# An MLP kernel whose first weight chunks work on two half blocks of tokens, with the LayerNorm statistics shared between two engines

## The chip, the cores and the metric

The kernel runs on one core of a Trainium2 chip. The metric is the time of one execution on the device, in microseconds (us), as the median of several executions. The engines are named as the profile names them: PE is TensorE, DVE is VectorE, ACT is ScalarE, POOL is GpSimd and SP is SyncE, which here only issues transfers.

## The reference

A block of a channel MLP: LayerNorm without gain or offset, a matrix product with W1, a bias and a tanh-approximated gelu, a second product with W2 and a bias. All inputs are bf16, with 2048 tokens, 1024 features and 3584 hidden features.

```python
def _layernorm(x, axis=-1, eps=1e-5):
    m = jnp.mean(x, axis=axis, keepdims=True)
    v = jnp.var(x, axis=axis, keepdims=True)
    return (x - m) / jnp.sqrt(v + eps)

def reference(x, w1, b1, w2, b2):
    y = _layernorm(x, axis=-1)
    h = _gelu(jnp.einsum("bsd,df->bsf", y, w1) + b1)
    return jnp.einsum("bsf,fd->bsd", h, w2) + b2
```

## The kernel before

The tokens are worked on in two blocks of 1024. Both matrix products use Strassen's scheme in Winograd's form: a product of 2 x 2 sub-matrices takes seven half-size products in place of eight, at the price of sums of the operands (S1 to S4 of the input, T1 to T4 of the weights), which DVE makes, and of sums of the results. A small list scheduler in the kernel file assigns a fixed order to each engine when the program is built; the priorities in the code are the scheduler's, and the chip runs the resulting order.

Before PE can work on the first block, each of its eight tiles of 128 tokens must go through this chain: load, statistics and scaling on DVE (with a power on POOL), eight transposes on PE, two copies out of PSUM by ACT.

```python
        def ln(s, i, prio, gate=()):
            st = [add("DVE", 0.68, lambda e, k=k: e.bn_stats(st_sb[:, i, 6 * k:6 * k + 6],
                                                             x_sb[:, i, k * HT:(k + 1) * HT]),
                      (x_ld[(s, i)][k], *gate), prio + 0.001 * k, f"st{s}_{i}_{k}") for k in range(2)]
            ag = add("DVE", 0.21, lambda e: e.bn_aggr(mv_sb[:, i, :], st_sb[:, i, :]), st, prio + 0.002, f"mv{s}_{i}")
            vp = add("DVE", 0.15, ...)                       # variance + eps
            rs = add("POOL", 0.55, ... op=ALU.pow ...)       # to the power -1/2
            y_ok[(s, i)] = add("DVE", 0.56, ...)             # (x - mean) * rstd, in fp16
```

The sums of the input combine tokens 0 to 511 with tokens 512 to 1023 (A1x and A2x below), so S1 to S4 wait for the last tile. Until then PE can do only the products that need no sum, P1 = A11 x W1 quarter and P2 = A12 x W1 quarter, and the kernel does them tile by tile for three units of 256 hidden features and whole for two more.

```python
            S1 = tt("S1", "A21", "A22", ALU.add, a21 + a22, ())
            S2 = tt("S2", "S1", "A11", ALU.subtract, a11, (S1,))
            S3 = tt("S3", "A11", "A21", ALU.subtract, a11 + a21, (S1,))
            S4 = tt("S4", "A12", "S2", ALU.subtract, a12, (S2,))
        # ...
                if p in (1, 2) and s == 0 and u < WAVE_UNITS:
                    o = None
                    for t in range(TH):
                        # 4 matmuls of 128 columns as soon as tile t is there
        # ...
        for i in range(NT):
            ln(0, i, -100 + 2.3 * i)
            pe_T(0, i, -60 + 2.3 * i)
```

Of the kernel before, what the change touches and what calls it, by code (L numbers as in the profile page):

```python
# [22 lines left out]
LN_EPS = 1e-5  # L23
# [7 lines left out]
OPEN_UNITS = 5  # L31
WAVE_UNITS = 3

MM512 = 0.2163
MM128 = 0.0585
# [35 lines left out]
class Planner:  # L71
# [3 lines left out]
    SLACK = {"PE": 0.35, "ACT": 0.1, "DVE": 0.1, "POOL": 0.1, "SP": 0.05}  # L75
# [9 lines left out]
    def place(self):  # L85
# [12 lines left out]
        while left:  # L98
# [46 lines left out]
            for u in o.users:  # L145
                u.waiting -= 1
                u.ready = max(u.ready, o.end + LAT)
                if u.waiting == 0:
                    avail.append(u)
# [43 lines left out]
def bass_standalone__mixer_channel_mlp__prompt_kernel(  # L193
# [24 lines left out]
    with ExitStack() as es:  # L218
# [47 lines left out]
        T_HEAD = 16.0  # L266
# [25 lines left out]
        def load_w1(s, c, prio):  # L292
            n = s * NC + c
            deps = w1_use.get(n - N_W1, ())
            w1_ld[(s, c)] = [dma(w1_sb[:, n % N_W1, j * KH:(j + 1) * KH, :],
                                 w1v[:, j * KH:(j + 1) * KH, c * 4 * P:(c + 1) * 4 * P], deps, prio + 0.01 * j,
                                 f"w1_{s}_{c}_{j}", f"w1_{n % N_W1}_{j}", KH * P * 4 * P * 2) for j in range(2)]
# [17 lines left out]
        load_x(0, 0, (), 0.0, halves=True, eng=("SP", "ACT"))  # L315
        load_x(0, 1, (), 0.1, halves=True, eng=("ACT", "ACT"))
        load_x(0, 2, (), 0.2)
        b1_ld = dma(b1r_sb[:, :], b1.rearrange("(t p) -> t p", p=P), (), 0.3, "b1", "b1", F * 2)
        load_w1(0, 0, 0.4)
        load_x(0, 3, (), 0.5)  # L320
        load_w1(0, 1, 0.6)
        for i in range(4, NT):
            load_x(0, i, (), 0.7 + 0.01 * i)
        load_w1(0, 2, 0.9)
        b2_ld = dma(b2_sb[:, :], b2.partition_broadcast(P), (), 30.0, "b2", "b2", P * D * 2)


        def warm(n, deps, prio):
# [5 lines left out]
        add("ACT", 1.3, lambda e: e.preload_act_table(ACT.Gelu_apprx_tanh), (), 1.0, "table")  # L334
# [3 lines left out]
                                                    identity=identb[0:FT, 0:FT]), ())], (c_idb, b1_ld), -4.0, "b1t",  # L338
                  alloc=hold_b)
        b1c = add("ACT", 0.2, lambda e: e.copy(out=b1_sb[:, :], in_=ps16[:, hold_b.k, 0:FT].bitcast(BF16)), (b1t,), 2.0,  # L340
                  "b1c", frees=(hold_b,))


        y_ok = {}
        x_free = {}

        def ln(s, i, prio, gate=()):
# [4 lines left out]
            vp = add("DVE", 0.15, lambda e: e.tensor_scalar(out=vpe_sb[:, i:i + 1], in0=mv_sb[:, i, 1:2],  # L352
# [8 lines left out]
            return st  # L361

# [5 lines left out]
        def pe_T(s, i, prio, gate=()):  # L368
# [7 lines left out]
            for k in range(2):  # L376
                res.append(add("ACT", 0.59, lambda e, k=k: e.copy(  # L377
                    out=dst_y(i, k), in_=ps16[:, hold.k, k * HT:(k + 1) * HT].rearrange("p (j s) -> p j s", j=KH)),
                    (tr, *gate), prio + 0.05 * k, f"te{s}_{i}_{k}", frees=(hold,) if k else ()))
            res[1].deps.append(res[0])  # L380
            y_in[(s, i)] = res

        def dma_T(s, i, prio, gate):
            res = []
            for k in range(2):
                res.append(add("SP", 0.45, lambda e, k=k: e.dma_start_transpose(
                    dst_y(i, k), x16[:, i, k * HT:(k + 1) * HT]), (y_ok[(s, i)], *gate[k]), prio + 0.05 * k,
                    f"yt{s}_{i}_{k}", sem=f"d_yt{i}{k}", inc=16, nbytes=P * HT * 2))
# [3 lines left out]
        ys = {}  # L392

        def y_sums(s, prio, gate=()):

            t1 = [y_in[(s, i)] for i in range(TH)]
            t2 = [y_in[(s, i)] for i in range(TH, NT)]
            a11, a12 = [[t[k] for t in t1] for k in range(2)]
            a21, a22 = [[t[k] for t in t2] for k in range(2)]

            def tt(n, x0, x1, op, deps, dp):
                res = []
                for g in range(2):
                    sl = slice(g * KH // 2, (g + 1) * KH // 2)
                    res.append(add("DVE", 0.62, lambda e, sl=sl: e.tensor_tensor(  # L405
                        out=yop[n][:, sl, :], in0=yop[x0][:, sl, :], in1=yop[x1][:, sl, :], op=op),
                        [*deps, *gate] + [d[g] for d in dp], prio + {"S1": 0, "S2": 1, "S3": 2, "S4": 3}[n] + 0.1 * g,
                        f"y{n}_{s}_{g}"))
                return res

            S1 = tt("S1", "A21", "A22", ALU.add, a21 + a22, ())
            S2 = tt("S2", "S1", "A11", ALU.subtract, a11, (S1,))
            S3 = tt("S3", "A11", "A21", ALU.subtract, a11 + a21, (S1,))
            S4 = tt("S4", "A12", "S2", ALU.subtract, a12, (S2,))
            rep = lambda l: [l[0]] * (KH // 2) + [l[1]] * (KH - KH // 2)
            ys[s] = {"S1": rep(S1), "S2": rep(S2), "S3": rep(S3), "S4": rep(S4)}
            for n, l in (("A11", a11), ("A12", a12), ("A22", a22)):
                ys[s][n] = l
# [6 lines left out]
        p_op = {}  # L425
        h_ok = {}
        c21_ok = {}
# [6 lines left out]
        def w1_sums(s, c):  # L434
            n = s * NC + c
            prio = base1[s] + c * 14 * SLOT - 2 * SLOT
# [15 lines left out]
        def mm1_unit(s, c, v, T, gate):  # L452
            n = s * NC + c
            u = 2 * c + v
            g = s * NU + u
            t0 = base1[s] + c * 14 * SLOT + v * SLOT
# [3 lines left out]
            pt = {p: t0 + 2 * k * SLOT for k, p in enumerate(SEQ1)}  # L460

            def prod(p, deps):
                yo, wo = OPER1[p]
                yd = ys[s][yo] if yo[0] == "S" else None
                lim = [c21_ok[g - OPEN_UNITS]] if p == 1 and g - OPEN_UNITS in c21_ok else []
                wd = [w1_ld[(s, c)][wo[0]]] if isinstance(wo, tuple) else [T[wo]]
                first = p in (1, 2, 5)
                if isinstance(wo, tuple):
                    lhs = lambda k: w1raw(n, wo[0], wo[1], v)[:, k, :]
                else:  # L470
                    lhs = lambda k: t1_sb[:, n % 2, wo - 1, k, v * P:(v + 1) * P]
                if p in (1, 2) and s == 0 and u < WAVE_UNITS:
                    o = None
                    for t in range(TH):
                        fn = [(lambda e, k=k, t=t: e.matmul(  # L475
                            ps[:, hold[p].k, t * P:(t + 1) * P], lhsT=lhs(k), rhs=yop[yo][:, k, t * P:(t + 1) * P],
                            start=(k == 0 and t == 0), stop=(k == KH - 1), skip_group_check=True), ())
                            for k in range(KH)]
                        yi = y_in[(s, t)][p - 1]
                        o = add("PE", KH * MM128, fn, [*deps, *wd, yi] + ([o] if o else []),  # L480
                                -5 + 2.3 * t + 0.1 * u + 0.01 * p, f"P{p}_{s}_{u}w{t}",
                                alloc=hold[p] if t == 0 else None)
                else:
                    if yd is None:
                        yd = [None] * KH
                        extra = ys[s][yo]
                    else:
                        extra = []
                    fn = [(lambda e, k=k: e.matmul(ps[:, hold[p].k, :], lhsT=lhs(k), rhs=yop[yo][:, k, :],  # L489
                                                   start=(first and k == 0), stop=(k == KH - 1),  # L490
                                                   skip_group_check=True), [d for d in (yd[k],) if d is not None])
                          for k in range(KH)]
                    o = add("PE", KH * MM512, fn, [*deps, *wd, *extra, *lim, *gate] + [d for d in yd if d is not None],
                            pt[p], f"P{p}_{s}_{u}", alloc=hold[p] if first else None)
                p_op[(s, u, p)] = o
                return o

            def bias(e_):
                return b1_sb[:, 2 * u + e_:2 * u + e_ + 1]

            def snap(p, o, hold_s, at):
# [4 lines left out]
                o_ = add(("ACT", "DVE"), {"ACT": 0.66, "DVE": 0.68}, fn, (o,), at, f"sn{p}_{s}_{u}", alloc=hold_s)  # L506
                return o_

            def fin(p, o, so, hold_s, at, frees):
                return add("DVE", 0.69, lambda e: e.tensor_tensor(  # L510
                    out=sn_sb[:, hold_s.k, :], in0=ps[:, hold[p].k, :], in1=sn_sb[:, hold_s.k, :], op=ALU.add),
                    (o, so), at, f"c{p}_{s}_{u}", frees=frees)

            def gelu(q, src, o, at, frees):
                e_ = q % 10 - 1
                h_ok[(s, q, u)] = add("ACT", 0.70, lambda e: e.activation(  # L516
                    out=h[q][:, u, :], in_=src(), func=ACT.Gelu_apprx_tanh, bias=bias(e_), scale=1.0),
                    [o, b1c, *h_war.get((s, q), ())], at, f"g{q}_{s}_{u}", frees=frees)
                return h_ok[(s, q, u)]

            sn = lambda hs: (lambda: sn_sb[:, hs.k, :])
# [16 lines left out]
            c21_ok[g] = gelu(21, lambda: ps[:, b0.k, :], P4, pt[4] + 4 * SLOT, (b0,))  # L538
            w1_use[n] += [P1, P2, P3]
            t1_use.setdefault(n, {})  # L540
            for p, k in ((5, 1), (6, 2), (7, 3), (4, 4)):
                t1_use[n].setdefault(k, []).append(p_op[(s, u, p)])
# [3 lines left out]
        h_war = {}  # L546
# [21 lines left out]
        def mm2_block(s):  # L568
# [8 lines left out]
            A = {q: (h[q], [[h_ok[(s, q, u)]] for u in range(NU)]) for q in h}  # L577
# [76 lines left out]
        for i in range(NT):  # L654
            ln(0, i, -100 + 2.3 * i)
            pe_T(0, i, -60 + 2.3 * i)
        for s in range(NSB):
            if s == 0:
# [82 lines left out]
```

## Time and profile before

| | before |
|---|---|
| median time | 364.64 us (three runs, 364.5 to 365.34) |
| span of the profiled run | 361.8 us |
| PE, DVE, ACT busy | 349.5, 244.4, 126.1 us |
| PE without a hole from | 33.10 us |
| DVE busy between 4 and 40 us | 33.2 of 36 us |

The span runs from the first to the last instruction of the profiled execution. PE is busy for 97% of it and has no hole after 33.10 us, so the figure that matters is what PE had not done by then. Over the whole 4 to 40 us this row shows who was at work in the opening (stretch, its length, then busy us of PE, weight loads, DVE, ACT and POOL with the number of instructions, the recorded clock of PE, the DMA share and GB/s). The prediction shows the other lines.

```profile
4.00:40.00 36.00, 27.71 (x229) 17.36 (x230) 33.22 (x71) 20.24 (x36) 4.37 (x8) 0.91 0.94 313
```

DVE is at work for 92% of that stretch, ACT for 56%.

### The profile page before, as it was taken

To read this page: it belongs to the slowest core of one execution; us is meant where nothing else is said; L and a number is where in the kernel's file an instruction comes from. 1 tells how busy PE (TensorE), PEld (TensorE's weight loads), DVE (VectorE), ACT (ScalarE), POOL (GpSimd) and SP (SyncE) were. 2 spreads that over 40 slices of the span, in tenths; PEclk is the share of its full clock that TensorE was granted. 3 is DMA by queue.
4 is the path that set the end of the run, shared out by engine and by line. 5 is a ranking of instruction groups with operands and counts; after the bars stand their busy time and mean duration, and the time that the engine had idled before them with its cause. 6 is when DMAs were issued, how large, how long until landed. Compare 5 with 4: busy or idle time off the path is not lost.

```text
span 361.8 us, 4463 instructions
## 1 busy us (share of the span) xinstructions
PE 349.5 (97%) x1731; PEld 164.2 (45%) x1731; DVE 244.4 (68%) x418; ACT 126.1 (35%) x200; POOL 10.1 (3%) x24
## 2 busy tenths in 40 slices
PE   4969999999999999999999999999999999999996
PEld 3843444444444444444444444444444444444442
DVE  5989998988963964983365566657443856797322
ACT  1584766776650000000006677667763000000000
POOL 2210000001100000000000000000000000000000
PEclk8799999999999999999999999999999999999999
DMA  8997333312349200046359330330005610001111
GB/s 265 363 349 274 116 117 118 116 17 102 116 133 349 71 29 2 0 92 120 95 190 317 119 116 11 108 116 2 1 0 192 216 43 16 0 0 45 43 43 43
DMA packets 45359, 40.39 MB, mean 112 GB/s; under 512 B 10139, under 2 KB 43419, under 8 KB 45339
## 3 DMA queue, kind: packets, MB, share of 16 engines
q1 hardware_dynamic: 44906, 39.73, 35.5%
q10 hardware_dynamic: 432, 0.39, 0.3%
q8 instruction: 13, 0.21, 0.2%
q14 instruction: 8, 0.06, 0.0%
HBM read 33.82 MB, written 4.19 MB: 105 GB/s over the span
## 4 chain that ended last, share of the span: by engine, by line
PE 93%; DVE 3%; ACT 2%; DMA 1%; issue 0%; SPq 0%
PE ps L612 47%; PE ps L489 43%; PE ps L475 2%; ACT yw_sb L377 1%; PE ps L370 1%; DVE yw_sb L405 1%; DMA x_sb<-in_x_dram 1%; DVE st_sb L348 1%; ACT h_sb L516 0%; DVE o_sb L584 0%; DVE sn_sb L510 0%; DVE t_sb L442 0%; ACT sn_sb L505 0%; DVE x_sb L358 0%; SPq L274 0%
## 5 line engine op out<-in xcount | busy, mean ns | idle before, releaser
L489 PE MATMUL ps<-yw_sb,t_sb 128*128 128x512 f16 x448 | 103.4, 379 | 0.4 <-DVE sn_sb L510 0.4
L612 PE MATMUL ps<-w2a_sb,h_sb 128*128 128x512 bf16 (+1 forms) x448 | 97.3, 379 | 0.0
L505 ACT COPY sn_sb<-ps 128x512 f32<-128x512 f32 x70 | 41.0, 588 | 109.5 <-PE ps L489 109.5
L489 PE MATMUL ps<-yw_sb,w_sb 128*128 128x512 f16 x312 | 74.2, 379 | 1.2 <-ACT yw_sb L377 1.2
L612 PE MATMUL ps<-yw_sb,h_sb 128*128 128x512 f16 (+1 forms) x336 | 72.8, 379 | 0.0
L516 ACT ACTIVATE h_sb<-sn_sb,b_sb 128x512 f16<-128x512 f32 x84 | 59.7, 719 | 24.6 <-DVE sn_sb L510 20.2
L489 PEld LDWEIGHTS ps<-yw_sb,t_sb 128*128 128x128 f16 x448 | 43.3, 98 | 54.3 <-ACT sn_sb L505 1.2
L612 PEld LDWEIGHTS ps<-w2a_sb,h_sb 128*128 128x128 f16 x448 | 43.7, 98 | 53.0 <-DVE o_sb L584 0.5
L510 DVE TENSOR_TENSOR sn_sb<-ps,sn_sb 128x512 f32<-128x512 f32 x84 | 56.6, 688 | 15.0 <-PE ps L489 14.3
L612 PEld LDWEIGHTS ps<-yw_sb,h_sb 128*128 128x128 f16 x336 | 32.9, 98 | 39.6
L489 PEld LDWEIGHTS ps<-yw_sb,w_sb 128*128 128x128 bf16 x312 | 30.2, 98 | 37.9 <-issue 1.9
L559 DVE TENSOR_TENSOR h_sb<-h_sb 128x1024 f16<-128x1024 f16 x56 | 35.8, 682 | 2.4 <-ACT h_sb L516 2.4
L584 DVE TENSOR_TENSOR sn_sb<-ps,b_sb 128x512 f32<-128x512 f32 x24 | 16.6, 690 | 25.4 <-PE ps L612 25.4
L442 DVE TENSOR_TENSOR t_sb<-w_sb,t_sb 128x1024 f16<-128x1024 bf16 x28 | 19.2, 687 | 13.6 <-PE ps L489 13.4
L584 DVE TENSOR_TENSOR o_sb<-ps,sn_sb 128x512 bf16<-128x512 f32 x24 | 16.5, 688 | 17.0 <-PE ps L612 16.9
L442 DVE TENSOR_TENSOR t_sb<-w_sb 128x1024 f16<-128x1024 bf16 x28 | 19.0, 682 | 8.5 <-PE ps L489 8.5
L348 DVE BATCH_NORM_STATS2 st_sb<-x_sb 128x6 f32<-128x512 bf16 x32 | 20.9, 673 | 4.4 <-DMA x_sb<-in_x_dram 4.4
L516 ACT ACTIVATE h_sb<-ps,b_sb 128x512 f16<-128x512 f32 x28 | 19.1, 682 | 1.6 <-PE ps L489 1.6
L405 DVE TENSOR_TENSOR yw_sb<-yw_sb 128x1024 f16<-128x1024 f16 x16 | 10.0, 683 | 10.0 <-DMA yw_sb<-x_sb 8.6
L584 DVE TENSOR_TENSOR o_sb<-ps,b_sb 128x512 bf16<-128x512 f32 x8 | 5.4, 688 | 12.6 <-PE ps L612 12.6
L377 ACT COPY yw_sb<-ps 128x512 f16<-128x512 f16 x16 | 9.2, 588 | 9.2 <-PE ps L370 9.0
L505 DVE COPY sn_sb<-ps 128x512 f32<-128x512 f32 x14 | 9.7, 691 | 3.7 <-PE ps L489 2.8
(26 smaller groups left out, 91.9 us busy)
## 6 DMA issues: line engine op xcount, KB each, us to landing
w_sb<-in_w_dram SPq DMA_DIRECT2D x28, 512.0 KB, 4.8
w2a_sb<-in_w_dram SPq DMA_DIRECT2D x4, 1792.0 KB, 12.0
yw_sb<-in_w_dram SPq DMA_DIRECT2D x4, 1792.0 KB, 11.8
out_dram<-o_sb SPq DMA_DIRECT2D x32, 128.0 KB, 1.7
x_sb<-in_x_dram SPq DMA_DIRECT2D x14, 256.0 KB, 7.7
x_sb<-in_x_dram ACTq DMA_DIRECT2D x3, 128.0 KB, 3.4
b_sb<-in_b_dram SPq DMA_DIRECT2D x1, 256.0 KB, 9.1
yw_sb<-x_sb SPq DMA_TRANSPOSE x16, 2.5
```

The source lines that it names most:

```text
L348: st = [add("DVE", 0.68, lambda e, k=k: e.bn_stats(st_sb[:, i, 6 * k:6 * k + 6], x_sb[:, i, k * HT:(k + 1) * HT]), (x_ld[(s, i)][k], *gate ...
L377: res.append(add("ACT", 0.59, lambda e, k=k: e.copy(out=dst_y(i, k), in_=ps16[:, hold.k, k * HT:(k + 1) * HT].rearrange("p (j s) -> p j s" ...
L405: res.append(add("DVE", 0.62, lambda e, sl=sl: e.tensor_tensor(out=yop[n][:, sl, :], in0=yop[x0][:, sl, :], in1=yop[x1][:, sl, :], op=op), ...
L442: return add("DVE", 0.65, lambda e: e.tensor_tensor(out=tv(k), in0=x0, in1=x1, op=ALU.subtract), [*deps, *war.get(k, ())], prio + 0.5 * k, ...
L475: fn = [(lambda e, k=k, t=t: e.matmul(ps[:, hold[p].k, t * P:(t + 1) * P], lhsT=lhs(k), rhs=yop[yo][:, k, t * P:(t + 1) * P], start=(k == ...
L489: fn = [(lambda e, k=k: e.matmul(ps[:, hold[p].k, :], lhsT=lhs(k), rhs=yop[yo][:, k, :], start=(first and k == 0), stop=(k == KH - 1), ski ...
L505: return e.copy(out=dst, in_=src) if o_.eng == "ACT" else e.tensor_copy(dst, src)
L510: return add("DVE", 0.69, lambda e: e.tensor_tensor(out=sn_sb[:, hold_s.k, :], in0=ps[:, hold[p].k, :], in1=sn_sb[:, hold_s.k, :], op=ALU. ...
L516: h_ok[(s, q, u)] = add("ACT", 0.70, lambda e: e.activation(out=h[q][:, u, :], in_=src(), func=ACT.Gelu_apprx_tanh, bias=bias(e_), scale=1.0),
L559: o = add("DVE", 0.63, lambda e, k0=k0, k1=k1: e.tensor_tensor(out=dst[:, k0:k1, :], in0=a[0][:, k0:k1, :], in1=b[0][:, k0:k1, :], op=op), ...
L584: return add("DVE", 0.69, lambda e: e.tensor_tensor(out=dst(), in0=ps[:, hold[p][t].k, :], in1=in1(), op=ALU.add), [m2[(p, t)], *deps], at ...
L612: fn = [(lambda e, k=k, t=t: e.matmul(ps[:, hold[p][t].k, :], lhsT=a[0][:, k, t * P:(t + 1) * P], rhs=b[0][:, k, :], start=(first and k == ...
```

## The change

The intent is to let PE begin with complete Strassen products before all eight tiles are there. For the first two chunks of W1 (each has 512 hidden features, two units), the first block is treated as two sub-blocks of 512 tokens, each with its own 256-token halves. The first sub-block needs only tiles 0 to 3. Its sums are kept for the time being in parts of the hidden buffer that are not yet used. Both units of a chunk share one PSUM bank, with 256 columns each. The later chunks still use the full block. Further, the statistics of tiles 1, 3, 5 and 7 go to ACT, the small additions to POOL, tiles 4 and 5 are transposed by DMA instead of PE, the copies of transposes may go to ACT or DVE, and the loads stand in one queue in the order in which they are used. Some planning constants of the scheduler and the gates of later loads changed as well (`SLACK` of ACT and DVE from 0.10 to 0.15, among others); no run below takes these back.

Some words of this text: the head is the work of the two split chunks; head sums are S1 to S4 of a sub-block, which I also call a half; raw products are P1 and P2, which need no sum; result sums are DVE's additions of finished products; the border is the passage of PE from the first sub-block to the second.

```diff
+LN_ACT = (1, 3, 5, 7)
+DMA_T = (4, 5)
+N_HEAD = 2
+HEAD_K = 10
-        T_HEAD = 16.0
+        T_HEAD = 13.3
 # ... loads
-        load_x(0, 1, (), 0.1, halves=True, eng=("ACT", "ACT"))
-        load_x(0, 2, (), 0.2)
-        b1_ld = dma(...)
-        load_w1(0, 0, 0.4)
-        load_x(0, 3, (), 0.5)
-        load_w1(0, 1, 0.6)
-        for i in range(4, NT):
-            load_x(0, i, (), 0.7 + 0.01 * i)
+        for i in range(1, TH):
+            load_x(0, i, (), -390 + 0.1 * i)
+        load_w1(0, 0, -380)
+        b1_ld = dma(...)
+        load_x(0, TH, (), -370)
+        load_x(0, TH + 1, (), -369)
+        load_w1(0, 1, -360)
+        load_x(0, TH + 2, (), -350)
+        load_x(0, TH + 3, (), -349)
 # ... statistics on ACT
+        def ln_act(s, i, j, prio):
+            a0 = add("ACT", 1.17, lambda e: e.activation(out=junk, in_=x_sb[:, i, :], func=ACT.Identity,
+                                                         accum_out=mv_sb[:, i, 0:1]), ...)
+            a1 = add("ACT", 0.2, lambda e: e.mul(mv_sb[:, i, 1:2], mv_sb[:, i, 0:1], -1.0 / D), ...)
+            a2 = add("ACT", 1.27, lambda e: e.activation(out=junk, in_=x_sb[:, i, :], func=ACT.Square,
+                                                         bias=mv_sb[:, i, 1:2], scale=1.0,
+                                                         accum_out=st_sb[:, i, 0:1]), ...)
 # ... copies of transposes on ACT or DVE
-                res.append(add("ACT", 0.59, lambda e, k=k: e.copy(...)))
+                res.append(add(("ACT", "DVE"), {"ACT": 0.6, "DVE": 0.44}, fn, ...))
 # ... the sums of a sub-block
+        def y_head(b, prio):
+            i0, hn = b * TH, TH // 2
+            src = {f"A{a}{k + 1}": (yop[f"A{b + 1}{k + 1}"][:, :, (a - 1) * HT // 2:a * HT // 2],
+                                    [y_in[(0, i)][k] for i in range(i0 + (a - 1) * hn, i0 + a * hn)])
+                   for a in (1, 2) for k in range(2)}
+            u0 = HEAD_K + 2 * b
+            dst = {n: h_sb[:, j, u0:u0 + 2, :]... for j, n in enumerate(("S1", "S2", "S3", "S4"))}
 # ... the main loop
+        for b in range(2):
+            for c in range(N_HEAD):
+                m = mm1_job(0, c, b, (0, 1), HEAD[b], T_c[c], base1[0] + (14 * b + c) * SLOT)
+        y_full(0, base1[0] + 14 * SLOT, (), raw + hb_ops)
```

## The prediction

> **What bounds the kernel now.** I read the page's busy row first (PE 97% of a span of 361.8 us), then the chain of waits in order of time, to see where the 3% that PE is not busy lies. The lines that matter are in the first 34 us:
>
> ```profile
> 1.25 3.83 DMA x_sb<-in_x_dram
> ...
> 24.71 0.48 ACT yw_sb L377
> 25.19 0.62 ACT h_sb L516
> 25.81 0.48 ACT yw_sb L377
> ...
> 26.94 2.57 DVE yw_sb L405 x5
> 29.50 0.45 issue
> 29.95 1.89 DVE yw_sb L405 x3
> 31.84 0.60 DVE t_sb L442
> 32.44 0.61 DVE sn_sb L510
> 33.05 0.05 issue
> 33.10 71.93 PE ps L489 x332
> 105.03 84.61 PE ps L612 x392
> ```
>
> From 33.10 us on, the chain is matmuls alone to 358.86; before it, it hops between DMA, DVE, ACT and PE. The sums of the transposed input (L405) begin only at 26.94, when the last of eight tiles has been normalised, transposed and copied out by ACT. Three stretches cut at those two times (columns: stretch, length, then busy us of each engine and instructions, clock, DMA share, GB/s):
>
> ```profile
> 0.00:33.10 33.10, 23.73 (x223) 16.99 (x224) 27.17 (x61) 15.83 (x29) 5.35 (x16) 0.90 1.01 335
> 33.10:358.86 325.76, 325.75 (x1508) 147.19 (x1508) 216.53 (x357) 110.26 (x172) 4.77 (x8) 1.00 0.30 90
> ```
>
> After 33.10, 1508 matmuls of 512 columns run without a hole, 325.76/1508 = 0.216 us each. The program needs 2 blocks x (14 x 7 x 4 + 4 x 7 x 14) = 1568 of them, so 60 (13.0 us) were done before. Hence the opening loses 33.10 - 13.0 = 20.1 us against a PE that had worked from the start. That number, the **lost head**, is all that this change can shorten. PE's 23.7 busy us there hide it: they hold 26 warm-up matmuls, 64 transposes, and work at half clock.
>
> What fills the opening is DVE: 27.2 busy of the 29.6 us from its first instruction at 3.55. Its groups before 33.1 us:
>
> ```profile
> L348 DVE BATCH_NORM_STATS2 st_sb<-x_sb 128x6 f32<-128x512 bf16 x16 | 10.4, 674 | 4.4 <-DMA x_sb<-in_x_dram 4.4
> L405 DVE TENSOR_TENSOR yw_sb<-yw_sb 128x1024 f16<-128x1024 f16 x8 | 4.9, 683 | 1.4 <-ACT yw_sb L377 1.4
> L358 DVE TENSOR_SCALAR x_sb<-x_sb,mv_sb,rstd_sb 128x1024 f16<-128x1024 bf16 x8 | 4.2, 538 | 0.1
> ```
>
> ACT is busy for 15.8 of 33 us only, so it has room. DVE instructions overlap a little: eight sums take 4.90 us (26.94 to 31.84), 0.61 each, and I charge such start-to-start costs below.
>
> **What the Trainium skill says.** "TensorE: Matmul & The Clock Gate", Part 1 (the HAM clock gate): an idle window of about 3.4 us halves the clock and a busy one restores it. The trace agrees: PE idles almost wholly from 3.98 to 8.2, and microsecond by microsecond (columns as above) the clock is still half at the end of steady work that began at 10.0, and full after it:
>
> ```profile
> 12.00:13.00 1.00, 1.00 (x12) 1.00 (x11) 0.98 (x4) 0.73 (x3) 0.14 (x1) 0.50 1.06 389
> 14.00:15.00 1.00, 1.00 (x21) 1.00 (x19) 1.00 (x4) 0.00 (x0) 0.00 (x0) 0.98 1.09 359
> ```
>
> "VectorE: DVE Perf Modes", the perf-mode tier table: tensor_tensor on 16-bit SBUF data reaches twice, never four times, the base rate. The trace fits: 1024 elements take 683 ns, where 0.96 GHz at one element a cycle would be 1067. So the new sums of 4 x 256 columns should cost what the old pieces of 2 x 512 do. "ScalarE: Activation LUTs", What ACT_TABLE_LOAD costs: 186 ns + 0.833 ns per element, 93 ns more for each pointer operand. Trace: 512-element copies 588 to 595 ns (613 by that sum), gelus 682 to 728 (707). "DMA: Bandwidth & Descriptors", Issuing engines are not separate DMA queues: loads started by several engines interleave on the same 16 engines. Trace: tile 1's first half, issued by ACT second, lands only about 5.07, with 0.9 MB moved.
>
> **The change part by part.**
> *Statistics.* Four tiles leave DVE: 8 bn_stats x 0.61 = 4.9, 4 aggregates about 0.5, and the small adds of all eight tiles (to POOL) about 0.5: -5.9 us DVE. ACT gets a sum (186 + 0.833 x 1024 = 1.04), a small multiply (0.2) and a square with pointer bias (1.13): 2.4 us x 4 = 9.5 us (estimate from the skill's formula; the change's own planning costs say 10.6).
> *Head sums.* Eight new sums of 1024 elements: +8 x 0.61 = 4.9 us DVE, and the eight full sums remain. Copies of transposes that now may go to DVE add about 4 x 0.45 = 1.8. Net DVE load: -5.9 + 4.9 + 1.8 = +0.8, thus nothing gained in load. The gain must come from order.
> *Transposes of tiles 4, 5 by DMA.* -16 PE transposes, -4 ACT copies (2.4 us); two pairs of transfers that took 2.5 us to land in the trace, late in a queue already drained.
> *256-column matmuls.* 112 matmuls of 512 become 224 of 256. At N/2.4 + 2.5 ns (the TensorE page; its 215.8 for 512 matches 0.216) they cost 224 x 0.109 = 24.4 against 24.2: +0.3. Gelus of these chunks become 32 short ones, 0.49 for 16 x 0.72: some +2 us on ACT.
> *Loads.* From the trace, landing is about 3.4 us + MB/0.365 (0.13 MB at 3.55; tile 3, 2.1 MB in, at 9.1). In the new order: tile 0 at 4.0, tile 1 4.8, 2 5.5, 3 6.2 (was 9.1), W1 chunk 0 at 7.7 and 9.1, chunk 1 at 12.0 and 13.4, tile 7 14.9.
>
> *The new opening.* Tile 0: statistics 3.6 to 5.2, POOL to 6.0, scaled by 6.7 (was 8.15). ACT does tile 1 from 4.8 to 7.4 and tile 3 to 10.1; DVE does tile 2 in between. Tile 3 is scaled near 11.6, transposed at half clock (0.9) by 12.5, copied by 13.4. The four first-half sums run 13.4 to 15.9. Meanwhile products 1 and 2 of chunk 0 (1.7 us of work) have run on tiles 0 and 1. PE can be continuous from about 13.4, when chunk 1's weights come too. The four head jobs are 24.2 us of matmul, 22.5 of them left: lossless they end at 35.9, so a lost head of 11.7.
> Losses on top, all estimates: with only two jobs open, a product waits for its PSUM copy (PE end to ACT end near 0.8 us, before a product of 0.87): 1.0. Between the halves DVE owes about 2.4 (chunk 1's sums) + 4.5 (rest of tiles 4 to 7) + 3.7 (six finishing adds at 0.61) + 2.4 (second head sums) = 13 us after 15.9, thus to 29, whereas the first half feeds PE to 23.8 and the second's raw products to 27.3: 1.3. Half clock reaching past 13.4: 0.8. Short matmuls 0.3. ACT, with about 33 us of work before 36, delaying copies: 0.4. Together 3.8, so a lost head of 15.5 and a gain of 20.1 - 15.5 = 4.6 us. All after that is unchanged, so 364.64 - 4.6 = **360.0 us**.
>
> **The rivals.** (1) *DVE remains the bound and the order gains little.* DVE was 92% busy from 3.55 to 33.1 and is full to 40 in the before trace, and its load does not fall. The change's own planned start moves from 16.0 to 13.3, only 2.7. Then 361.5 to 363. Against: DVE's old work was wholly ahead of products that need sums; half of it now is not. (2) *ACT takes its place.* Statistics of 2.4 us in one go ahead of a PSUM copy stall PE, and gelus hold snapshot slots. For: +9.5 us on ACT just when copies are due. Against: it was idle for half the opening. 362 to 365. (3) *Everything overlaps as planned*: no loss between the halves, the clock up by 13.4: lost head 12.5, 357.0, over 2%. (4) *Tables*: if the sum or square forced table loads at 1.28 us each (the trace's one load), +5 us. Against: the preload is made once and the copies beside gelus now cause no second one.
>
> **Range and chances.** 2% is 7.3 us, a lost head below 12.9, close to my lossless 11.7, so faster needs nearly all to fit: 0.17. Slower needs a head of 27: 0.03. Within 2%: 0.80. Range 356.8 (gaps of 0.6) to 363.3 (gaps of 7).
>
> **What would show it.** PE continuous from about 36 or earlier, with some 83 to 96 512-equivalents done by then; the lost head computed the same way near 15.5; first head sum near 13.4; tile 3 landing near 6.2; DVE busy over 90% from 4 to 40; ACT near 135 us in all (126 before); clock full by 14 to 15. A first head sum after 15, a PE hole over 2 us between the halves, a second ACT table load, or holes after 40 us would make the prediction wrong.

## The result

The changed kernel takes 359.15 us (median of four runs, 358.75 to 361.28), against 364.71 us of the kernel before in the same rounds (364.5 to 365.34). A ratio in this text is the mean time of one kernel's fast runs over that of the kernel before in the same rounds, so it is not quite the ratio of the medians. Here it is 0.9857, with a 95% interval of 0.9816 to 0.9897: 1.4% faster, which is clear of the noise and inside the 2% that counts as the same. The predicted 360.0 us with its range of 356.8 to 363.3 holds it.

The chain of waits of the changed kernel, in order of time (start, length, what ran):

```profile
5.37 7.48 DMA w_sb<-in_w_dram
12.85 0.05 issue
12.90 0.62 PE ps L529 x8
13.52 0.46 PE ps L397 x8
13.98 0.02 issue
14.01 0.59 ACT yw_sb L406
14.62 0.59 ACT yw_sb L406
...
15.31 0.70 DVE h_sb L433
...
24.51 0.55 DVE x_sb L362
25.05 0.05 issue
25.10 0.62 PE ps L397 x8
25.72 1.03 PE ps L529 x8
26.75 0.45 PE ps L397 x8
27.19 73.53 PE ps L529 x400
100.73 84.61 PE ps L672 x392
```

The second stage (L672) starts at 100.73 us instead of 105.03. The matmuls of the first stage of a whole block take 84.61 us when nothing interrupts them, as they do in the second block (the chain of either kernel has that line). The time in the first block that PE did not spend on such work was therefore 105.03 - 84.61 = 20.4 us and is 100.73 - 84.61 = 16.1 us. The difference of 4.3 us is the whole difference of the two spans, 361.8 and 357.5. Nothing else moved. The profiled execution of the kernel before was one of its faster ones, which is why the medians are 5.6 us apart and the traces 4.3.

The same stretches as in the prediction, cut where PE becomes continuous (columns as there), and then 4 to 40 us:

```profile
0.00:27.19 27.19, 19.62 (x213) 17.09 (x214) 21.44 (x41) 19.78 (x39) 8.70 (x24) 0.94 0.56 173
27.19:354.56 327.37, 327.36 (x1577) 153.63 (x1574) 225.61 (x371) 112.39 (x188) 4.76 (x8) 1.00 0.36 110
...
4.00:40.00 36.00, 29.54 (x300) 25.48 (x301) 33.32 (x62) 28.88 (x62) 7.73 (x16) 0.95 0.65 210
```

DVE had to do 21.4 us of work before PE could run on, instead of 27.2. Between 4 and 40 us it is as busy as before, 33.3 against 33.2 us. The order is new: part of what stood ahead of PE's start now runs beside it. ACT went from 20.2 to 28.9 us there, and from 126.1 to 132.2 us in all. The groups before 27.19 us, DVE first, then ACT (busy us and mean ns behind the bar, then idle time and its releaser):

```profile
L352 DVE BATCH_NORM_STATS2 st_sb<-x_sb 128x6 f32<-128x512 bf16 x8 | 5.3, 686 | 4.4 <-DMA x_sb<-in_x_dram 4.4
L406 DVE COPY yw_sb<-ps 128x512 f16<-128x512 f16 x4 | 1.7, 424 | 0.4 <-PE ps L397 0.3
L433 DVE TENSOR_TENSOR h_sb<-yw_sb 128x1024 f16<-128x1024 f16 x2 | 1.4, 688 | 0.3 <-ACT yw_sb L406 0.3
...
L374 ACT ACTIVATE h_sb<-x_sb,mv_sb 128x1024 f16<-128x1024 bf16 x4 | 4.6, 1149 | 0.1
L370 ACT ACTIVATE h_sb<-x_sb 128x1024 f16<-128x1024 bf16 x4 | 4.2, 1054 | 1.9 <-DMA x_sb<-in_x_dram 1.9
L370 ACT ACTIVATION_READ_ACCUMULATOR h_sb<-x_sb 128x1 f32 x4 | 0.8, 189 | 0.0
```

The statistics on DVE halved from 16 to 8 instructions, and the 8 full sums are no longer among what PE waits for. Most of what is left of the lost head is the time up to 12.90, when PE had done only 1.7 us of useful work, and a hole of 1.9 us from 23.2 to 25.1 us between the sub-blocks, when DVE has not yet finished the first half's result sums and the second half's tiles.

### The profile page after: what moved, and what is told of

Its sections match the earlier page's. It is cut to its first block, busy times and chain, and to the rows that moved or that the text cites. A ratio compares the mean times of both kernels' runs of the same rounds, so it can differ in the third digit from the quotient of the medians.

```text
span 357.5 us, 4613 instructions
## 1 busy us (share of the span) xinstructions
PE 347.0 (97%) x1787; PEld 170.7 (48%) x1787; DVE 247.7 (69%) x412; ACT 132.2 (37%) x226; POOL 13.5 (4%) x32
## 4 chain that ended last, share of the span: by engine, by line
PE 92%; DVE 2%; DMA 2%; SPq 1%; POOL 0%; issue 0%; ACT 0%; DVEq 0%
PE ps L672 47%; PE ps L529 45%; DMA w_sb<-in_w_dram 2%; SPq L278 1%; DVE h_sb L433 1%; DVE st_sb L352 1%; PE ps L397 0%; ACT yw_sb L406 0%; DVE x_sb L362 0%; POOL rstd_sb L359 0%; DVE o_sb L644 0%; DVE sn_sb L557 0%; DVE t_sb L487 0%; POOL vpe_sb L356 0%; DVE x_sb L384 0%
## 5 line engine op out<-in xcount | busy, mean ns | idle before, releaser
L672 PE MATMUL ps<-w2a_sb,h_sb 128*128 128x512 bf16 (+1 forms) x448 | 97.3, 379 | 0.0
L529 PE MATMUL ps<-yw_sb,t_sb 128*128 128x512 f16 (+1 forms) x416 | 92.8, 371 | 0.0
L552 ACT COPY sn_sb<-ps 128x512 f32<-128x512 f32 x70 | 40.6, 586 | 105.2 <-PE ps L529 105.1
L529 PE MATMUL ps<-yw_sb,w_sb 128*128 128x512 f16 (+2 forms) x384 | 76.9, 346 | 1.0 <-DVE yw_sb L406 0.6
L672 PE MATMUL ps<-yw_sb,h_sb 128*128 128x512 f16 (+1 forms) x336 | 72.8, 379 | 0.0
L566 ACT ACTIVATE h_sb<-sn_sb,b_sb 128x512 f16<-128x512 f32 (+1 forms) x96 | 61.8, 666 | 25.1 <-DVE sn_sb L557 20.9
L672 PEld LDWEIGHTS ps<-w2a_sb,h_sb 128*128 128x128 f16 x448 | 43.7, 98 | 53.0
L557 DVE TENSOR_TENSOR sn_sb<-ps,sn_sb 128x512 f32<-128x512 f32 x84 | 56.5, 687 | 15.8 <-PE ps L529 14.8
L529 PEld LDWEIGHTS ps<-yw_sb,t_sb 128*128 128x128 f16 x416 | 40.5, 98 | 45.9 <-DVE sn_sb L557 0.2
L529 PEld LDWEIGHTS ps<-yw_sb,w_sb 128*128 128x128 bf16 x384 | 35.2, 99 | 35.6 <-DMA w_sb<-in_w_dram 1.4
L672 PEld LDWEIGHTS ps<-yw_sb,h_sb 128*128 128x128 f16 x336 | 32.8, 98 | 39.7
L487 DVE TENSOR_TENSOR t_sb<-w_sb,t_sb 128x1024 f16<-128x1024 bf16 x28 | 19.3, 689 | 12.1 <-PE ps L529 11.7
L566 ACT ACTIVATE h_sb<-ps,b_sb 128x512 f16<-128x512 f32 (+1 forms) x32 | 19.7, 628 | 3.5 <-PE ps L529 3.5
L352 DVE BATCH_NORM_STATS2 st_sb<-x_sb 128x6 f32<-128x512 bf16 x24 | 16.2, 685 | 4.4 <-DMA x_sb<-in_x_dram 4.4
L552 DVE COPY sn_sb<-ps 128x512 f32<-128x512 f32 x14 | 9.6, 690 | 3.7 <-PE ps L529 3.0
L529 PE MATMUL ps<-h_sb,t_sb 128*128 128x256 f16 x96 | 11.2, 273 | 0.5 <-DVE h_sb L433 0.5
L359 POOL TENSOR_TENSOR rstd_sb<-vpe_sb,nhalf 128x1 f32<-128x1 f32 x12 | 7.3, 611 | 76.7 <-DVE vpe_sb L356 76.4
```

The source lines that it names most:

```text
L359: rs = add("POOL", 0.55, lambda e: e.tensor_tensor(out=rstd_sb[:, i:i + 1], in0=vpe_sb[:, i:i + 1], in1=nhalf[:, :], op=ALU.pow), (vp, c_n ...
L487: return add("DVE", 0.65, lambda e: e.tensor_tensor(out=tv(k), in0=x0, in1=x1, op=ALU.subtract), [*deps, *war.get(k, ())], prio + 0.5 * k, ...
L529: return lambda e: e.matmul(ps[:, hold[p].k, j * W + a:j * W + b], lhsT=lhs(v, k), rhs=rhs[:, k, a:b], start=(first and j == k == a == 0), ...
L552: return e.copy(out=dst, in_=src) if o_.eng == "ACT" else e.tensor_copy(dst, src)
L557: return add("DVE", 0.69, lambda e: e.tensor_tensor(out=sn_sb[:, hold_s.k, :], in0=ps[:, hold[p].k, :], in1=sn_sb[:, hold_s.k, :], op=ALU. ...
L566: fn.append((lambda e, j=j, u=u, f=f: e.activation(out=h[hq][:, u, c0:c0 + W], in_=src(j * W, (j + 1) * W), func=ACT.Gelu_apprx_tanh, bias ...
```

## The experiments

Twelve kernels ran, in three groups, each group on one chip beside the kernel before; the changed kernel has rounds of its own, so kernels of different groups are compared by their ratios. All gave correct results. My theory was that DVE's order and DVE's load act together: the split lets PE start sooner, and the statistics on ACT let DVE reach the second half in time. The rivals were that one of the two does everything. Times are medians.

| run | what differs | us | ratio to before |
|---|---|---|---|
| changed kernel | | 359.15 | 0.9857 |
| e1_stats_dve | split kept, statistics on DVE | 365.11 | 1.0006 |
| e2_no_split | no split, the rest kept | 362.20 | 0.9936 |
| e3_pe_transposes | tiles 4, 5 transposed on PE | 359.43 | 0.9856 |
| e4_old_loads | loads as before | 359.68 | 0.9863 |
| e9_hole_filled | e1 and matmuls in the hole | 362.82 | 0.9953 |
| e7_warm | 74 warm-up matmuls | 359.31 | 0.9859 |
| e5_w1_first | W1 chunk 1 loaded earlier | 360.81 | 0.9880 |
| e6_ln4_early | tile 4 earlier in DVE's order | 358.98 | 0.9845 |
| e8_one_chunk | one chunk split, not two | 359.50 | 0.9849 |
| e11_fill | matmuls in the hole | 360.01 | 0.9868 |
| e12_w1_fill | e5 and e11 | 360.17 | 0.9873 |
| e13_five_act | e12 and tile 6 on ACT | 360.90 | 0.9903 |

The half-widths of the 95% intervals are 0.0015 to 0.0025 for most runs, about 0.003 for e5 and e13 and 0.004 for the changed kernel.

### e1_stats_dve and e2_no_split: each half of the change alone

```diff
# e1_stats_dve
-LN_ACT = (1, 3, 5, 7)
+LN_ACT = ()
# e2_no_split
-N_HEAD = 2
+N_HEAD = 0
-                if p in (1, 2) and key == 0:
+                if p in (1, 2) and (key == 0 or s == 0 and 2 * c + vs[0] < 3):
-        y_head(0, 9)
-        T = w1_sums(0, 0, 8)
-        T_c[1] = w1_sums(0, 1, 13)
-        hb_ops = y_head(1, 23)
# and: T_HEAD, the priorities of tiles 4 to 7, of the full sums and of W1 chunk 2 as in the kernel before
```

> Split kept, all statistics of block 0 back on DVE. Mine (order and load act together): the first half hardly suffers, DVE can do four tiles by about 12, but about 5 us of DVE work return to the stretch between the halves, where PE already has a hole (23.2 to 25.1 us); the hole grows by 2 to 3 us: about 361.5 us, half of the gain lost. Rival (the gain is the relief of DVE alone): about 364.5. Rival (the gain is the split alone): 359.2, as the changed kernel.

> The split taken out (full 1024-token products with the old wave order for three units), with statistics on ACT, the new load order and the new transposes kept. Mine: the eight full sums must again wait for tile 7, but DVE reaches it some 3 us sooner: about 362.5 us. Rival (relief of DVE is all): 359.5. Rival (the split is all): 364.7, as before.

Without the split the kernel gains 2.2 us in the medians (364.43 to 362.20), as expected. With the split and without the statistics on ACT it gains nothing, 365.11 us, which is 3.6 us worse than I expected. Both together gain 5.6. So the number of one rival came out (364.5), but its claim did not: if the relief of DVE were everything, the run without the split would have shown 359.5. As they stand, the two parts need each other; how much of that is the clock of PE is shown below. Both runs keep the new load order, the DMA transposes and the free choice of engine for the copies, and a kernel with these alone was not run.

Why e1 lost so much shows in its matmuls in order of time (start, length, engine, line, shapes, number, and in brackets the idle time before and its releaser):

```profile
23.24 1.04 PE L529 MATMUL ps<-h_sb,w_sb 128*128 128x256 f16 x8
28.02 1.04 PE L397 MATMUL ps<-ident,x_sb 128*128 128x128 f16 x8 [3.74 <-DVE x_sb L362]
28.85 1.91 PE L529 MATMUL ps<-yw_sb,t_sb 128*128 128x256 f16 x8
30.55 3.39 PE L529 MATMUL ps<-yw_sb,w_sb 128*128 128x256 f16 x16
33.78 1.04 PE L529 MATMUL ps<-yw_sb,t_sb 128*128 128x256 f16 x8
34.65 0.61 PE L397 MATMUL ps<-ident,x_sb 128*128 128x128 f16 x8
```

The first half suffered more than I expected (its first product with a head sum starts at 17.12 us, in the changed kernel at 16.06), and the hole between the sub-blocks grew from 1.9 to 3.7 us, a little less than expected. But after it, eight transposes take 1.04 us instead of the 0.61 of 34.65 us, and eight 256-column matmuls 1.91 us instead of 1.04: PE worked at half its clock for nearly 6 us, from 28.0 to 33.7.

The trace of e2 has the same in a smaller size (columns as above):

```profile
22.16 1.22 PE L397 MATMUL ps<-ident,x_sb 128*128 128x128 f16 x16 [2.38 <-DVE sn_sb L557]
24.17 3.43 PE L529 MATMUL ps<-yw_sb,w_sb 128*128 128x512 f16 x8 [0.79 <-ACT yw_sb L406]
27.43 6.42 PE L529 MATMUL ps<-yw_sb,t_sb 128*128 128x512 f16 x28
33.78 1.90 PE L529 MATMUL ps<-yw_sb,w_sb 128*128 128x512 f16 x8
35.51 6.21 PE L529 MATMUL ps<-yw_sb,t_sb 128*128 128x512 f16 x28
```

After a hole of 2.38 us and a wait of 0.79, eight matmuls of 512 columns take 3.26 us to the start of the next group (24.17 to 27.43), where the eight from 33.78 take 1.73. So up to 1.5 us of e2's time is half clock. This is an estimate: no run filled that hole, and the full sums, on which DVE works until 30.1 us, might have become the next wait.

### e9_hole_filled: the clock measured by itself

```diff
 # on top of e1
                 raw.append(m[1])
+                if (b, c) == (0, 1):
+                    warm(40, (m[3], m[7]), 20.0)      # 40 matmuls of ones, result unused
```

> The run with all statistics on DVE, plus 40 matmuls of ones (128 columns, about 2.2 us at full clock) on PE where its trace has the 3.7 us hole between the halves. The useful work and its order are the same. Mine: in that run half of the loss is the clock, halved from 26.9 to 33.7 us after the hole (6.8 us at half speed, 3.4 us lost); with the hole filled the clock stays up: 365.1 - 3.4 = 361.7 us. Rival (the whole loss is DVE work that comes too late): 365.1 or more, as without the filling.

The median is 362.82 us. The matmuls of the same stretch:

```profile
24.34 2.40 PE L334 MATMUL ps<-ones 128*128 128x128 f16 x40
28.25 0.62 PE L397 MATMUL ps<-ident,x_sb 128*128 128x128 f16 x8 [1.51 <-DVE x_sb L362]
28.84 1.05 PE L529 MATMUL ps<-yw_sb,t_sb 128*128 128x256 f16 x8
29.73 1.91 PE L529 MATMUL ps<-yw_sb,w_sb 128*128 128x256 f16 x16
31.47 1.04 PE L529 MATMUL ps<-yw_sb,t_sb 128*128 128x256 f16 x8
32.35 0.61 PE L397 MATMUL ps<-ident,x_sb 128*128 128x128 f16 x8
```

The useful work starts at the same time (28.25, in e1 28.02), but from there to tile 7's transposes it takes 4.1 us instead of 6.6. The 2.5 us agree with the 2.3 us between the medians (1.9 by the ratios, 1.0006 and 0.9953). So of the 6 us that e1 lost against the changed kernel, some 2.3 were the clock. The rest goes with the statistics that stayed on DVE: tile 6's transposes start at 28.02 us in place of 25.10. I had expected 3.4 for the clock, because I had counted all 6.8 us of half clock; PE had work in only the 5.7 us from 28.0 to 33.7, and half of that is 2.8.

This changes how the first two runs are read. With the hole filled, the split alone gains 1.7 us (364.51 to 362.82); without its half clock, e2 would gain up to 3.7. That makes up to 5.4 of the 5.6 us of both together. So the two parts may nearly add up, and most of their need for each other be the clock: either part alone leaves a hole after which the clock halves. For e1 this is measured, for e2 it is estimated.

### e3_pe_transposes and e4_old_loads: the smaller parts

```diff
# e3_pe_transposes
-DMA_T = (4, 5)
+DMA_T = ()
# e4_old_loads: order x0, x1 (halves, on two queues), x2, b1, W1 chunk 0, x3, W1 chunk 1, x4 to x7
```

> Tiles 4 and 5 transposed on PE again, copied by ACT or DVE. Mine: the DMA transposes are a small help, the hole between the halves is set by DVE (statistics of tile 4 late), so within 0.6 us of the changed kernel, 359.2 to 359.8. Rival (the DMA transposes themselves, issued from 21.6 over 5.2 us, make the hole): 357.5 to 358.

> Loads of the opening in the order and on the queues of the kernel before, the rest as changed. Mine: tile 3 lands near 9 instead of about 6.3, its ACT statistics begin 2 us later, the first head sum moves from 15.3 to about 17, and the end with it by about 1.5: 360.7 us. Rival (the second W1 chunk, landing at 12.9, sets the start of PE's work and comes earlier in the old order): 358.8 or less.

Neither can be told from the changed kernel (0.9856 and 0.9863 against 0.9857). For e3 this is what I expected. The rival, that the DMA transposes make the hole, is right about the hole and wrong about the time: in e3's trace the hole is filled with the 16 transposes and raw products, and PE's longest wait after 13 us is 0.56 us, but from the first product with a head sum to the end it takes 356.6 - 15.04 = 341.6 us, and the changed kernel 357.5 - 16.06 = 341.4. (That trace is e3's fastest run, 358.32 us, with an earlier start.) For e4 I had expected 1.5 us more. Its chain shows why nothing came of it (its lines are numbered one lower than the changed kernel's):

```profile
17.19 0.70 DVE h_sb L432
17.89 0.05 issue
17.94 7.16 PE ps L528 x64
25.10 0.55 PE ps L396 x8
...
26.68 0.45 PE ps L396 x8
27.12 32.96 PE ps L528 x212
```

The first head sum did move from 15.31 to 17.19 us, as expected. Yet tile 6's transposes start at about 25.1, now without a wait, and PE is continuous from 27.1 us, as in the changed kernel. DVE had scaled tile 6 by 24.98 us, in the changed kernel by 25.05. What PE lost before the first sum it did not lose in the hole between the sub-blocks, because the border between them is set by how far DVE has come, not by PE.

### e7_warm, e5_w1_first, e6_ln4_early: earlier starts

```diff
# e7_warm
-N_WARM = 26
+N_WARM = 74
# e5_w1_first: load_w1(0, 1) ahead of load_x(0, 4) and load_x(0, 5)
# e6_ln4_early
-                ln(0, i, 14 + 3 * (i - TH))
+                ln(0, i, 7.0 if i == TH else 14 + 3 * (i - TH))
```

> The changed kernel with 74 instead of 26 warm-up matmuls, so that PE is busy until the first transposes near 7 us and these and the first products run at full clock. Mine: transposes of tiles 0 to 2 and raw products shorten by 0.4 to 1 us each, but the second W1 chunk (12.9) and tile 3's statistics set the first head sum, so only 0.3 us or so: 358.9 us. Rival (half clock until 10 to 13 us holds the first half back): 358 us or less.

> The changed kernel with W1 chunk 1 loaded ahead of tiles 4 and 5. Mine: in the trace PE stood behind chunk 1's products (12.90 to 13.36) with tile 3 already scaled at 12.63; chunk 1 lands 1.4 us earlier, tile 3's transpose goes 0.7 us earlier and with it the first sum, but the hole between the halves, set by DVE's queue, eats part: 358.7 us. Rival (the load is hidden behind DVE's chain): 359.2.

> The changed kernel with tile 4's statistics put ahead of the weight sums in DVE's order, so that the halves' border is reached earlier; the same work. Mine: the hole between the halves (1.9 us) shrinks by about 1: 358.2 us. Rival (DVE is saturated, so what goes first delays something else by as much): 359.2 or slower.

None beats the changed kernel clearly. In e7 the first transposes and products run at full clock (eight transposes 0.61 instead of 1.03 us), but PE then waits for the second W1 chunk until 13.72 us in that trace; the rival, 358 us or less, was wrong. e5 missed both my 358.7 us and the rival's 359.2 by its median. In the trace of one of its two fast runs (358.61 us) the earlier load did what I expected: tile 3's transposes, the first product with a head sum and tile 6's transposes all come 0.6 us earlier (12.75, 15.45 and 24.49 us against 13.36, 16.06 and 25.10), and the hole stays at 1.88 us. In e6 the hole before tile 6's transposes shrinks from 1.9 to 0.6 us, and waits of 1.0, 0.25 and 0.17 us for head sums appear earlier: the same DVE work in another order, 358.98 us. My expectation of 358.2 was wrong and the rival of a saturated DVE right.

The spread of these runs says more than their medians. e7 has five runs from 359.0 to 359.85 and one at 361.69; e5 has two at 358.06 and 358.61 and four from 360.79 to 361.72; the changed kernel has three near 359 and one at 361.28. The profiled execution of e7 is its slow one. Its stretches of a microsecond each, after the hole (columns as above; the clock is the third number from the end):

```profile
24.00:25.00 1.00, 0.04 (x1) 0.00 (x0) 0.97 (x4) 0.15 (x1) 0.57 (x2) 1.00 0.35 69
...
26.00:27.00 1.00, 1.00 (x12) 0.77 (x13) 1.00 (x3) 0.97 (x3) 0.00 (x0) 0.89 0.62 129
27.00:28.00 1.00, 1.00 (x7) 0.67 (x6) 1.00 (x2) 0.97 (x3) 0.00 (x0) 0.50 0.38 75
...
29.00:30.00 1.00, 1.00 (x7) 0.68 (x5) 0.85 (x2) 1.00 (x3) 0.00 (x0) 0.50 0.03 8
```

The same hole of 1.9 us (24.04 to 25.92) is followed here by half clock from about 26.9 to 30 us. From tile 6's transposes to the second half's first raw products this run takes 4.46 us (25.92 to 30.38), the changed kernel's trace 2.80 (25.10 to 27.90): 1.7 us. The late W1 chunk adds 0.8. Together they are the 2.5 us between 361.69 and 359.15. That the slow runs of e5 and of the changed kernel have the same cause is argued, not shown: no slow run of theirs was traced, and the trace of e11 below loses 1.7 us in another way.

### e11_fill, e12_w1_fill, e13_five_act: trying for a better kernel

```diff
# e11_fill: 24 matmuls of ones after the first half, as in e9
# e12_w1_fill: e5_w1_first and e11_fill
# e13_five_act: e12 and
-LN_ACT = (1, 3, 5, 7)
+LN_ACT = (1, 3, 5, 6, 7)
```

> The changed kernel with 24 matmuls of ones put into the hole between the halves; nothing else. The changed kernel's four runs lie at 358.75 to 359.18 and once at 361.28. Mine (the odd run is a halved clock after the hole, as the trace of the run with more warm-up matmuls shows from 26.5 to 30.4): all runs within 358.6 to 359.5, none above 360. Rival (the odd run has another cause): one in four still near 361.

> W1 chunk 1 loaded ahead of tiles 4 and 5, and the hole filled. Without the filling this order had runs at 358.06 and 358.61 and four at 360.8 to 361.7. Mine: the load order is worth 0.5 us and the clock took it away: all runs near 358.3. Rival (the order itself is slower): 360.8.

> As the run before in this list, and tile 6's statistics on ACT as well (1.4 us less on DVE, 2.4 more on ACT). Mine (DVE is what the border between the halves waits for, ACT still has room): 357.5 us, the hole under 1 us. Rival (ACT is full by now, its sums delay the PSUM copies): 358.5 or slower.

Both expectations for the filling failed. I expected e11 within 358.6 to 359.5 us, and it has 359.51 to 360.9 with a median of 360.01; I expected 358.3 for e12, and it has 360.17, near the rival's 360.8. None of their 11 runs is above 360.9 us, while one of four of the changed kernel and two of six of e5 are at or above 361.0; that is too few to show that the filling removes slow runs. In e11's trace (360.9 us) the border is late for another reason: PE's first products still ran at half clock until after 13 us (12 matmuls of 128 columns in each microsecond from 10 to 13, 22 in the one from 14), tile 3's transposes came at 14.13 instead of 13.36, the border 0.8 us later, and behind it PE waited 0.8 us for the DMA transposes, which start late with their tiles. Whether that is chance of this group of runs or has to do with the filling is open: the changed kernel was not run again on that chip.

e13 takes 360.9 us where I expected 357.5; whether it is slower than e12 the intervals do not tell (0.9903 and 0.9873). PE's waits in its trace, which is its fastest run (359.95 us), show why nothing was gained (who waited for whom: total us, times, longest):

```profile
PE ps L397 <- DVE x_sb L362: 3.1, 1, 3.1
PE ps L529 <- DVE sn_sb L552: 1.7, 1, 1.7
```

The 3.1 us are the start, before tile 0. The hole for tile 6 is gone, and a new wait of 1.7 us has come in its place: PE waits for a copy of a product out of PSUM (L552) which the scheduler had given to DVE, at 21.28 us. ACT was in the statistics of another tile until 20.6 us then, and in two other such copies after it. This is near the rival of the expectation, but the copy itself stood on DVE, behind the scaling of two tiles from 20.36 us on.

### e8_one_chunk: the size of the split

```diff
-N_HEAD = 2
+N_HEAD = 1
-        T_c[1] = w1_sums(0, 1, 13)
```

> The changed kernel with only the first W1 chunk over two sub-blocks instead of two chunks. Mine: the first half offers 6 us of matmul work instead of 12, so PE runs dry about 6 us sooner while DVE needs the same time to reach the second half and the full sums: a hole of 6 us or more, filled in part by raw products of other chunks (some 3.5 us), and the clock halves: 363 us. Rival (one chunk is enough, and halves the short gelus): 359 or less.

It takes 359.5 us, the same as with two chunks; I was wrong by 3.5 us. The trace has no large hole: PE's longest wait after the start is 1.6 us, for the first head sum of the second half at 26.7. The raw products of the full block for chunk 1 (16 matmuls of 512 columns, from 14.8, 18.3 and 20.9 us on) need only tiles 0 to 3 and stood in for the second split chunk. I had counted these 3.5 us of products. I had not considered that one split job less in the first half also means three result sums less, some 1.8 us by DVE's 0.61 each, ahead of the border; that this is the reason is argued, not tested. So the second chunk of the split buys nothing that these runs can tell.

## Why the prediction was right

**The frame held.** The prediction said that only the lost head can change and put it at 15.5 us after 20.1. Counted in its way, the changed kernel has 400 matmuls after 27.19 us, 280 of 512 columns and 120 of 256, or 340 equivalents of 392, so 52 were done before (11.2 us) and the lost head is 27.19 - 11.2 = 16.0 us. That is a gain of 4.1 us where 4.6 was predicted. The medians show 5.6, because the traced execution of the kernel before (363.54 us) was 1.1 us faster than its median.

**The load of DVE held.** The prediction has +0.8 us, so that "the gain must come from order". By the durations in the two traces the head sums brought 5.5 us and the copies 2.5, while statistics, aggregates and small additions took away 5.1, 0.7 and 1.1: +1.2 us. (DVE's busy time in all rose by 3.3 us, to 247.7. The 33.2 and 33.3 us between 4 and 40 show no load, since DVE is nearly full there in both.) The experiments qualify it. The head sums take back what the statistics gave; with the split in, leaving the statistics on DVE costs the whole gain (e1). The prediction had no term for what a longer hole does to the clock, and e9 measures it at 2.3 us.

**Statistics on ACT were undersized.** The prediction has 2.4 us a tile; they take 1.054 + 0.189 + 0.208 + 1.149 + 0.188 = 2.8 us. The two activations were right to 2%; reading the accumulator out is an instruction of its own, of 0.19 us, that I had not counted. Copies on DVE were six for four, at 0.424 us. The short gelus were undersized too: the prediction says "some +2 us", but its own figures give 32 x 0.49 - 16 x 0.72 = 4.2, and the durations of all gelus rose from 79.5 to 84.1 us. ACT's busy time of 132.2 us is still near the predicted 135.

**The step that failed** is "Tile 3 is scaled near 11.6 ... The four first-half sums run 13.4 to 15.9". The first sum ran at 15.31. Tile 3 was scaled by 12.63, since POOL took 1.3 us for it (0.8 for tile 1) and DVE was then copying transposes; its own transposes then stood in PE's order behind chunk 1's first products, which waited for their weights to 12.85. The prediction itself had listed "a first head sum after 15" among the signs that would make it wrong, so this part of its opening was wrong by its own test. The miss cost little: e4 made the same sum later still, 17.19 us, and kept the time. PE's start at "about 13.4" was right (12.90).

**The gaps.** Together predicted at 3.8 us on a lossless 11.7, they were 4.8 after 12.90 (14.29 us to 27.19, with 44 equivalents or 9.5 us done in it) on a lost 11.2 (12.90 less 1.7). The hole between the halves was 1.9 us where the prediction has 1.3 (its own figures, 29 and 27.3, give 1.7). The transposes of tiles 3, 6 and 7 on PE, 8 x 0.056 = 0.45 us each and 1.3 together, were missing from the sum. Half clock past the start (0.8) did not occur in the profiled run, which had full clock from about 10.7 us. The wait for PSUM copies (1.0) and ACT's delays (0.4) were not seen; PE waited 0.5 us for the first sum. What remains, about 1 us, I did not separate. That the total came within 1 us is in part luck: of the predicted 3.8, the 2.2 for half clock, PSUM copies and ACT were not seen, and the transposes, the longer hole and the wait for the first sum stood in for them. The short matmuls were right: 48 of 256 columns take 5.42 us, and less the last one's 0.27 that is 0.110 each.

**The rivals.** The first, that DVE remains the bound, has the right mechanism (e4 and e6 move work about and keep the time) and the wrong size. The second, ACT as the new bound, did not happen with four tiles; with five (e13) a wait of 1.7 us appeared, for a copy on DVE. The third, that everything overlaps with a lost head of 12.5 us, did not happen (16.0). Table loads did not happen: the trace has one.

## What to carry to other kernels

When an engine is busy throughout an opening and another waits for its results, look for the part of its work that the waiting engine does not need yet: the new order gained 5.6 us here with DVE's load no smaller, but only together with moving enough work away that the order could be kept. Count a hole of PE twice, once for its length and once for the clock after it: filling the 3.7 us hole of e1 with unused matmuls gained 2.3 us, filling the 1.9 us hole of the changed kernel gained nothing in the median. Before you say that two parts of a change need each other, look for half clock in the run of each part alone. Then try a smaller version of the change, since one split chunk did here what two do.

## What the Trainium skill lacked or had wrong

- "TensorE: Matmul & The Clock Gate", Why this matters for your kernels: it asks for no PE-idle gaps above about 3 us. In the traced slow run here (e7_warm) a hole of 1.88 us was followed by half clock from about 26.9 to 30 us, and in the changed kernel's trace a hole of the same length was not. In e2_no_split it followed a hole of 2.38 us and a wait of 0.79. So half clock can follow a hole shorter than the page's figure, in some executions, and cost 1.7 us in e7_warm; with the 3.74 us of e1_stats_dve it cost 1.9 to 2.5.
- The same page, Part 1, warns that the recorded clock events are not always to be trusted. These runs agree and give a size: e1_stats_dve's profile shows a clock of 1.00 at 12 to 13 us (its recorded clock events begin only at 13.09), while eight transposes at 12.08 took 1.06 us, against 0.62 at 14.11. The duration of a known matmul is the better witness.
- "ScalarE: Activation LUTs", What ACT_TABLE_LOAD costs: its formula gives 1.04 and 1.13 us for 1024 elements, and the trace 1.054 and 1.149. It lacks the price of an accumulator output: a second instruction of 0.189 us, each time.
- "GPSIMD Engine Reference", Specifications, says that POOL shares its SBUF interfaces with DVE and contends with two-input instructions. It gives no duration there: in the opening of the changed kernel the power on 128 x 1 elements took 0.55 to 0.57 us, and 0.86 to 0.88 us in the three cases in which it met sums of two SBUF operands on DVE.
